# Two loads on SyncE's queue change places: half of the first pair's gate logits and the whole of the second pair's

## The chip, the cores and the metric

The kernel runs on one core of a Trainium2 chip. The metric is the device time of one execution in microseconds (us), the median of several executions. The profile is one further execution, taken by the hardware profiler.

## The reference

The program computes a gated linear recurrence over 768 time steps for 4 batches of 8 heads with 48 channels each, and behind it an MLP mixer over tokens and channels with 384 columns. Cut to what matters:

```
f = 1.0 / (1.0 + np.exp(-f_logit))                    # (4, 8, 768, 48)
for t in range(S):
    state = f[:, :, t, :, None] * state + np.einsum('bhd,bhe->bhde', k[:, :, t], v[:, :, t])
    y[:, :, t] = np.einsum('bhd,bhde->bhe', q[:, :, t], state)
x = y.transpose(0, 2, 1, 3).reshape(B, S, H * D)      # (4, 768, 384)
h = np.maximum(x.transpose(0, 2, 1) @ w_tok1, 0.0) @ w_tok2
u = x + h.transpose(0, 2, 1)
out = u + np.maximum(u @ w_ch1, 0.0) @ w_ch2
```

All inputs and the output are float32.

## The kernel before

**Tiling.** A batch of 768 steps is cut into six chunks of 128 steps, and the chunks are taken in three pairs, P = 0, 1, 2. In a pair, partition q of a tile holds the two neighbouring steps 2q and 2q+1, so a load of one pair brings runs of 96 elements. For each pair the kernel takes the gate logits f to the logarithm of the gate, `log(1 + exp(-f))`, on ScalarE; for the first two pairs of batch 0 this is one activation with the softplus table (line 454, in place in `f_sb`), for all later pairs an Exp and a Ln (lines 457 and 459). VectorE adds the two steps of each partition (`two`, line 448). TensorE sums over the steps with a triangular matrix (`sums`, line 479), and, for batch 0, takes the totals of the two chunks (`totals`, line 486). VectorE takes `first` from the sums (line 499), ScalarE makes the factors `GG` by Exp (lines 502 and 519), and VectorE multiplies q and k by them (`qk`, line 448 too, since it is a line of a helper). Then TensorE turns q and k (line 546), makes state contributions (`parts`, line 599), scores (line 581) and outputs (lines 657 and 665). The mixer follows: token layers (lines 709 and 725) and channel layers (lines 784 and 803), which are most of TensorE's work.

**Loads of batch 0.** Five loads come through the queues of SyncE (SP) and ScalarE (ACT) or GpSimd (POOL) at the start:

- the logits of pair 0 in two halves of four heads: `load_half(0, SP)` (192 KB in the profile's KB, line 348, SyncE's queue) and `load_half(1, ACT)` (the same line, ScalarE's queue). Both write the first pair's part of the tile `f_sb`; the first softplus needs both;
- the logits of pair 1, `load("f", 0, 1, SP)` (384 KB, line 357, SyncE's queue). The second softplus needs it;
- the logits of pair 2, `load("f", 0, 2, SP)` (384 KB, line 357, SyncE's queue), which is held back by a memset on POOL (`mark`, line 342);
- q, k and v of the three pairs, then the weights, all issued by POOL (lines 357, 418, 364), with a conversion to bf16.

Below, f1 is the load of pair 1's logits, half 0 and half 1 are the two halves of pair 0's, and f2 is the load of pair 2's.

**Order.** Every step of the program is an `Op` in a list. `ORDER`, written out by hand, is the order in which a planner (`Plan.best`) goes over them; each entry is four times an Op's number plus the choice of its engine. Op 2 is half 0 (entry 8), Op 3 is half 1 (entry 12) and Op 5 is f1 (entry 20). On one engine the steps are issued in the order of `ORDER`. The planner gives each Op a time on a clock of its own, from constants in the code; a load through SyncE's queue or a half through ScalarE's counts as landed a fixed time behind its issue:

```
HELD = (3850, 4300, 7100)                             # halves of pair 0, pair 1, pair 2
...
if e == PE and free[PE] < until and t - free[PE] > 270:
    n = int(t / 410) if not free[PE] else int((t - free[PE] - 50) / 215)
```

The times of this clock, in ns, decide two things that are in the program itself: which of the eight PSUM banks a step takes (the one that has been free longest by that clock), and, by the lines above, how many filler matmuls (`idle(n)`, line 852) TensorE is given ahead of a step that the planner sees waiting. The first such group stands ahead of the first pair's `sums`. In `idle(n)`, every four units are one float32 matmul of 512 columns, which the profile shows as two instructions, and each unit left over is one bf16 matmul of 512 columns.

In the kernel before, the first group is 14 units: three float32 matmuls (six instructions) and two bf16 ones.

Of the kernel before, what the change touches and what calls it, by code (L numbers as in the profile page):

```python
# [20 lines left out]
TURNED = 2  # L21
NQ = 2
ORDER = (
# [862 lines left out]
```

## Time and profile before

| | |
|---|---|
| time, median of 3 runs | 167.19 us (167.08 to 167.43) |
| time of the profiled execution | 167.07 us |
| its span, first to last instruction | 165.4 us |
| outside its span | 1.67 us |
| TensorE busy | 159.7 us (97% of the span) |
| VectorE busy | 128.5 us (78%) |
| ScalarE busy | 106.7 us (65%) |
| GpSimd busy | 61.7 us (37%) |
| granted TensorE clock | 1.00 |

In the lines of the profile PE is TensorE, PEld its weight loads, DVE VectorE, ACT ScalarE, POOL GpSimd, SP SyncE; a name with q behind it is that engine's queue of issues and waits. L454 is line 454 of the kernel. A line of the timeline has the start in us from the span's start, the duration of the group in us, engine, line, operation, what it writes and reads, the count, and in brackets the idle time just before and what ended it. Instructions that overlap in a pipeline are merged in such a group; a window that starts inside the group shows the later ones by themselves.

### The profile page before, as it was taken

How to read it: one execution, taken by the hardware profiler on the slowest of the kernel's cores; microseconds unless marked ns; L12 is line 12 of the kernel's file. 1: busy time of each engine (PE TensorE's matmuls, PEld its weight loads, DVE VectorE, ACT ScalarE, POOL GpSimd, SP SyncE). 2: the span in 40 equal slices, each digit the busy share in tenths (PEclk: the TensorE clock that was granted, in tenths of full speed). 3: DMA queues.
4: the chain of work that ended last, by engine and by line, in shares of the span. 5: the costliest groups of instructions: out<-in, count | busy, mean ns of one | idle time of the engine just before them, and what ended most of it. 6: DMA issues, size and time to landing. Idle time of an engine off the chain costs nothing.

```text
span 165.4 us, 4992 instructions
## 1 busy us (share of the span) xinstructions
PE 159.7 (97%) x2053; PEld 101.8 (62%) x2053; DVE 128.5 (78%) x284; ACT 106.7 (65%) x231; POOL 61.7 (37%) x86
## 2 busy tenths in 40 slices
PE   7999998999999999999999999999999999999992
PEld 3276665566666776666566766665667656565661
DVE  6558997589999999998999999988599526704331
ACT  3599785797899999999949966384812511623300
POOL 7970799954778610003904515200322020000000
DMA  4999999999999999566999990991900030680406
GB/s 110 221 179 171 200 212 240 176 209 225 220 226 222 225 244 142 96 87 127 141 214 121 144 125 0 108 213 49 222 6 4 0 65 10 182 319 20 175 32 206
DMA packets 68183, 24.34 MB, mean 147 GB/s; under 512 B 60896, under 2 KB 67296, under 8 KB 68160
## 3 DMA queue, kind: packets, MB, share of 16 engines
q0 software_dynamic: 41856, 13.77, 68.9%
q1 hardware_dynamic: 25776, 10.06, 29.1%
q8 instruction: 16, 0.26, 0.6%
q10 hardware_dynamic: 528, 0.20, 0.4%
q14 instruction: 7, 0.06, 0.1%
HBM read 25.17 MB, written 4.72 MB: 181 GB/s over the span
## 4 chain that ended last, share of the span: by engine, by line
PE 84%; DVE 3%; ACT 2%; issue 1%; DVEq 0%
PE ps L803 29%; PE ps L784 28%; PE ps L709 5%; PE ps L725 4%; PE ps L665 4%; PE ps L581 3%; PE ps L657 3%; PE ps L546 2%; PE ps L599 2%; PE ps L852 1%; PE ps L766 1%; PE ps L481 1%; PE ps L482 1%; DVE AmT L624 1%; DVE qk L448 1%
## 5 line engine op out<-in xcount | busy, mean ns | idle before, releaser
L803 PE MATMUL ps<-w_ch,zT 128*128 128x384 bf16 (+2 forms) x300 | 53.9, 320 | 0.0
L784 PE MATMUL ps<-uT,w_ch 128*128 128x384 bf16 x288 | 51.6, 326 | 0.0
L784 PEld LDWEIGHTS <-w_ch 128*128 128x128 bf16 x288 | 27.8, 98 | 17.6
L803 PEld LDWEIGHTS <-zT 128*128 128x128 bf16 x300 | 28.0, 98 | 17.1
L443 ACT ACTIVATE zT<-ps 128x384 bf16<-128x384 f32 x57 | 25.1, 493 | 16.3 <-PE ps L784 16.1
L624 DVE TENSOR_TENSOR AmT<-ps,mask 128x512 bf16<-128x512 f32 x44 | 28.6, 683 | 1.5 <-PE ps L581 1.2
L445 DVE TENSOR_SCALAR zT<-ps 128x384 bf16<-128x384 f32 x39 | 20.6, 551 | 10.0 <-PE ps L784 9.3
L814 DVE TENSOR_TENSOR x_nat<-x_nat,ps 128x384 f32<-128x384 f32 (+2 forms) x25 | 13.1, 532 | 10.5 <-PE ps L803 10.5
L438 POOL CAST state_bd<-state 48x192 bf16<-48x192 f32 x15 | 5.7, 377 | 28.8 <-DVE state L641 26.1
L502 ACT ACTIVATE GG<-ps 128x384 bf16<-128x384 f32 x24 | 11.0, 485 | 3.6 <-DVE first L499 2.9
L448 DVE TENSOR_TENSOR qk<-qk_sb,GG 128x768 bf16<-128x768 bf16 x24 | 12.8, 560 | 0.0
L357 POOL DMA_DIRECT2D v_sb<-in_v_dram x12 | 10.7, 894 | 5.3 <-DMA w_ch<-in_moe_w_ch_dram 3.4
L852 PE MATMUL ps<-steady 128*128 128x512 f32 (+1 forms) x21 | 11.5, 669 | 1.2 <-DVE steady L372 1.0
L519 ACT ACTIVATE GG<-first 128x384 bf16<-128x384 f32 x24 | 11.7, 518 | 0.2
L434 ACT ACTIVATE x_bf<-ps 128x384 bf16<-128x384 f32 x15 | 6.9, 483 | 7.4 <-PE ps L657 7.1
L741 DVE TENSOR_TENSOR x_nat<-x_nat,ps 128x384 f32<-128x384 f32 x21 | 10.6, 548 | 1.4 <-PE ps L725 1.2
L357 POOL DMA_DIRECT2D qk_sb<-in_k_dram x12 | 10.9, 904 | 1.7 <-POOLq L870 0.8
L434 ACT ACTIVATE u_bf<-x_nat 128x384 bf16<-128x384 f32 x12 | 5.8, 518 | 8.6 <-DVE x_nat L741 8.6
L357 POOL DMA_DIRECT2D qk_sb<-in_q_dram x12 | 10.8, 898 | 0.5 <-DMA qk_sb<-in_q_dram 0.3
L438 POOL COPY qT<-qJ 128x1024 bf16<-128x1024 bf16 x3 | 3.4, 1146 | 18.6 <-ACT zT L443 18.6
L709 PE MATMUL ps<-x_bf,w_tok 128*128 128x384 bf16 x48 | 10.3, 327 | 0.0
L434 ACT ACTIVATE x_nat<-ps 128x384 f32<-128x384 f32 x20 | 9.3, 491 | 0.1
(87 smaller groups left out, 230.8 us busy)
## 6 DMA issues: line engine op xcount, KB each, us to landing
out_dram<-x_nat SPq DMA_DIRECT2D x23, 192.0 KB, 2.2
f_sb<-in_f_logit_dram POOLq DMA_DIRECT2D x9, 384.0 KB, 8.8
qk_sb<-in_k_dram POOLq DMA_DIRECT2D x12, 192.0 KB, 8.6
qk_sb<-in_q_dram POOLq DMA_DIRECT2D x12, 192.0 KB, 8.7
v_sb<-in_v_dram POOLq DMA_DIRECT2D x12, 192.0 KB, 8.9
w_ch<-in_moe_w_ch_dram POOLq DMA_DIRECT2D x2, 576.0 KB, 9.1
w_ch<-in_moe_w_ch_dram POOLq DMA_DIRECT2D x1, 1152.0 KB, 10.3
f_sb<-in_f_logit_dram SPq DMA_DIRECT2D x2, 384.0 KB, 5.8
```

Source lines behind the costliest of these rows:

```text
L357: lambda eng=eng, into=held(dst[i], P), of=runs(src, b, P): eng.dma_start(out=into, in_=of),
L434: nc.scalar.activation(out_, in_, AF.Copy, bias=0.0, scale=1.0)
L443: nc.scalar.activation(out_, in_, AF.Relu, bias=0.0, scale=1.0)
L445: nc.vector.tensor_scalar(out_, in_, 0.0, None, ALU.max)
L448: (nc.vector if op.engine == DVE else nc.gpsimd).tensor_tensor(out_, a, b_, what)
L519: add(ACT, r, lambda n=n: nc.scalar.activation(GG[i][:, 0, n], first[i], AF.Exp, bias=0.0, scale=2.0 * n - 1.0), need=[("first", i)] + ([" ...
L624: add(DVE, r, lambda into=into, made=made, m4=m4: nc.vector.tensor_tensor(into, made(), m4, ALU.mult), need=masks, make=[("AmT", i, js, pa ...
L709: add(PE, rank("tok1", rt), lambda rt=rt, kt=kt, pm=pm: nc.tensor.matmul(banks[pm.at][:, 0:DM], lhsT=w_tok1[:, kt, rt * 128:(rt + 1) * 128 ...
L784: nc.tensor.matmul(banks[pm.at][:, 0:384], lhsT=w[:, kt, c0:c0 + 128], rhs=uT[:, th, :, kt, :], start=(kt == 0), stop=(kt == 2))
L803: nc.tensor.matmul(banks[pm.at][:, 0:n1 - n0], lhsT=zT[:, kt, tt * 128:(tt + 1) * 128], rhs=w_ch2[:, kt, n0:n1], start=(kt == 0), stop=(kt ...
L814: add(DVE, rank("ch2", tt), lambda un=un, pm=pm, n=n1 - n0: nc.vector.tensor_tensor(un, un, banks[pm.at][:, 0:n], ALU.add), make=[("x_nat" ...
L852: nc.tensor.matmul(banks[NBANK - 1], lhsT=one.broadcast_to((128, 128)), rhs=one.broadcast_to((128, 512)), start=True, stop=True)
```

## The change

Entries 20 (f1) and 8 (half 0) of `ORDER` change places. SyncE's queue is then given half 0 first and f1 behind it. No other entry moves, and no load changes its size, its tile or its queue.

```
 ORDER = (
-    0, 4, 12, 16, 24, 28, 32, 20, 8, 188, 192, 196, 36, 40, 44, 76, 68, 48, 52, 60, 208, 356, 212, 220, 64, 224,
+    0, 4, 12, 16, 24, 28, 32, 8, 20, 188, 192, 196, 36, 40, 44, 76, 68, 48, 52, 60, 208, 356, 212, 220, 64, 224,
```

Since the planner goes over `ORDER`, its clock is worked out anew with the two loads in their new places.

## The prediction

> **What bounds the kernel now.** I read the table of busy time by stretch first, to see where a start that comes earlier could still be lost (columns: stretch, its length, busy us and instructions of PE, PEld, DVE, ACT, POOL, the granted clock, the DMA share, GB/s).
>
> ```profile
> 0.00:8.00 8.00, 6.98 (x10) 2.45 (x10) 4.96 (x27) 3.48 (x4) 6.81 (x14) 1.00 1.05 165
> 34.00:160.00 126.00, 126.00 (x1596) 80.59 (x1594) 102.25 (x212) 82.79 (x184) 35.32 (x51) 1.00 0.89 134
> ```
>
> From 34 to 160 us TensorE has no idle time: 126 us of 126. There the end is set by TensorE's work and by when that work begins, so whatever moves the state of the program at 34 us moves the end by as much. The question is what sets the time before 34.
>
> The timeline of the first 11 us answers it, engine by engine. First the three issues and ScalarE, with the time from issue to landing of the three loads from the DMA view (the second of its rows is half 0; the third, from a window that ends ahead of the other issues, is f1).
>
> ```profile
> 0.81 0.48 ACTq L348 DMA_DIRECT2D f_sb<-in_f_logit_dram  x1
> 0.81 0.47 SPq L357 DMA_DIRECT2D f_sb<-in_f_logit_dram  x1
> 1.34 0.60 SPq L348 DMA_DIRECT2D f_sb<-in_f_logit_dram  x1
> 5.79 1.58 ACT L454 ACTIVATE f_sb<-f_sb 128x768 f32<-128x768 f32 x2 [3.19 <-DMA f_sb<-in_f_logit_dram]
> 6.54 0.83 ACT L454 ACTIVATE f_sb<-f_sb 128x768 f32<-128x768 f32 x1
> 7.38 1.28 ACT L841 ACT_TABLE_LOAD   x1
> 8.82 0.49 ACT L502 ACTIVATE GG<-ps 128x384 bf16<-128x384 f32 x1 [0.15 <-DVE first L499]
> 9.20 0.93 ACT L519 ACTIVATE GG<-first 128x384 bf16<-128x384 f32 x2
> ```
> ```profile
> f_sb<-in_f_logit_dram ACTq DMA_DIRECT2D x1, 192.0 KB, 4.2
> f_sb<-in_f_logit_dram SPq DMA_DIRECT2D x1, 192.0 KB, 4.4
> f_sb<-in_f_logit_dram SPq DMA_DIRECT2D x1, 384.0 KB, 4.4
> ```
>
> Half 1 lands at 0.81 + 4.2 = 5.0, f1 at 0.81 + 4.4 = 5.2, half 0 at 1.34 + 4.4 = 5.74. The first softplus needs both halves and starts at 5.79, right behind half 0. The load that is needed first lands last, while f1, needed second, waits 0.54 us in the tile. ScalarE's 3.19 us of idle time end on that load.
>
> Then VectorE and TensorE behind it (the rows of TensorE are from windows that begin inside its groups, so that each start can be read).
>
> ```profile
> 6.66 0.56 DVE L448 TENSOR_TENSOR two<-f_sb 128x384 f32<-128x384 f32 x1 [1.22 <-ACT f_sb L454]
> 7.39 0.56 DVE L448 TENSOR_TENSOR two<-f_sb 128x384 f32<-128x384 f32 x1 [0.18 <-ACT f_sb L454]
> 8.22 0.56 DVE L499 TENSOR_TENSOR first<-ps,f_sb 128x384 f32<-128x384 f32 x1 [0.27 <-PE ps L479]
> 9.80 0.56 DVE L499 TENSOR_TENSOR first<-ps,f_sb 128x384 f32<-128x384 f32 x1 [0.91 <-PE ps L486]
> 10.27 1.02 DVE L448 TENSOR_TENSOR qk<-qk_sb,GG 128x768 bf16<-128x768 bf16 x2
> ```
> ```profile
> 0.99 6.26 PE L852 MATMUL ps<-steady 128*128 128x512 f32 x8 [0.99 <-DVE steady L372]
> 6.28 0.98 PE L852 MATMUL ps<-steady 128*128 128x512 bf16 x2
> 6.70 0.55 PE L852 MATMUL ps<-steady 128*128 128x512 bf16 x1
> 7.28 1.65 PE L479 MATMUL ps<-two,tri 128*128 128x384 f32 x4
> 7.70 1.22 PE L479 MATMUL ps<-two,tri 128*128 128x384 f32 x3
> 8.03 0.90 PE L479 MATMUL ps<-two,tri 128*128 128x384 f32 x2
> 8.44 0.49 PE L479 MATMUL ps<-two,tri 128*128 128x384 f32 x1
> 8.76 1.89 PE L486 MATMUL ps<-ones,two 128*128 128x64 f32 x16
> ```
>
> Two legs run to the first `qk` at 10.27. One: second softplus 6.54, `two` 7.39, sums of the second pair 8.03, its totals 8.76, its `first` 9.80, and `qk` 0.47 us behind it in VectorE's order. The other: table load to 8.66, GG at 8.82 behind the first pair's `first` (8.22), and the two Exps that end at 9.20 + 0.93 = 10.13. They meet within 0.14 us, so both must come earlier. From `qk` on the chain of waits runs through VectorE and ScalarE to TensorE's channel layers with no load named as a releaser.
>
> **The change part by part.** *The loads.* No byte and no issue is added; SyncE issues the same two loads, the second 0.5 to 0.6 us behind the first as now, and f2 behind them waits for POOL's memset either way. What moves is the order in which SyncE's queue (q1) is drained; ScalarE's is q10, POOL's q0. The DMA view for windows from 0 to 3.25, 4.5 and 5.25 gives packets so far:
>
> ```profile
> q1 hardware_dynamic: 419, 0.16, 26.5%
> q10 hardware_dynamic: 12, 0.00, 0.5%
> ...
> q1 hardware_dynamic: 993, 0.38, 36.6%
> q10 hardware_dynamic: 505, 0.19, 15.3%
> ...
> q1 hardware_dynamic: 1554, 0.59, 45.7%
> q10 hardware_dynamic: 528, 0.20, 13.6%
> q0 software_dynamic: 82, 0.02, 3.5%
> ```
>
> q10's 528 packets are all of half 1, so a half is 528 and f1 about twice that. In q1 the first 528 packets, now half 0's, are through between 3.25 and 4.5 (at an even pace 3.25 + 1.25 x 109 / 574 = 3.49); before, half 0 was the last third, through at about 5.3, and landed 0.45 us later. So half 0 will land at 3.9 to 4.2, ahead of half 1, whose queue I leave as it is: 5.0. The first softplus then starts at 5.0 + 0.05 = 5.05 in place of 5.79, a gain of 0.74. f1 becomes the last third: its last packets go at 5.3, and with a tail between 0.45 (half 0's) and 0.65 (f1's now: its packet 1040 at about 4.55, landing 5.2) it lands at 5.75 to 5.95. The second softplus can follow the first after the pitch 6.54 - 5.79 = 0.75, at 5.80; so it starts at 5.80 to 6.00 in place of 6.54. The gain there is 0.54 to 0.74 and cannot be more, since one softplus must still follow the last landing where two did.
>
> *The filler matmuls.* The wording hides a second edit. The planner's clock puts half 0 at 3850 in place of 4280, so its first softplus moves from 4318 to 3888, `two` from 5196 to 4766, and the first `sums` from 5801 to 5371; int(5371 / 410) = 13 where it was 14. This is a count written into the program, no time of the chip. Thirteen units are three float32 and one bf16 matmul: one bf16 filler less. It matters: with 14, TensorE would be in fillers until about 6.70 + 0.42 = 7.12 and the sums, at 7.28 now, would gain 0.16 at most. With 13 they can start at 6.70. On paper the clock's lead of 430 is 195 at the second pair's sums, 10 at the first `parts` (values taken as landed at 10350) and 74 behind; the next two filler counts stay at 4 (4.50 before rounding in both) and 8 (8.87 and 8.56), and the bank picks that I followed, to 17 us of that clock, stay. Later picks may differ: bounded by one eviction more or less in a row of two, 0.5 us to either side (the 0.49 of the GG row), taken as 0 because a pick by longest-free seldom binds.
>
> *The sums.* The first pair's `two` would start at 5.05 + (6.66 - 5.79) = 5.92 and end at 6.48, so the sums would start when the fillers are done, 6.70, a gain of 0.58. Two bounds for the rest. The granted clock reads 1.00 in the first 8 us, but the fillers' pace does not bear it out: the bf16 filler at 6.28 took 0.42 to the next. The four float32 pieces of the sums take 0.42, 0.33, 0.41, 0.32: the first piece of each pair is the long one, whichever pair it is, so by 7.28 the array was at its full pace already, and up to 6.70 it ran at about half pace (a float32 filler piece took about 0.88, six of them from 0.99 to 6.28; the two at 10.49, quoted next, took 1.08 together). The switch lay between 6.70 and 7.28. At 6.70: the pieces start at 6.70 and 7.12 and the second pair's at 7.45. At 7.28: the first piece does 0.58 / 0.84 of its work by 7.28 and ends at 7.41, the second at 7.74. The second pair's sums, at 8.03 now, so start at 7.45 to 7.74, a gain of 0.29 to 0.58 (`two` is there by 7.45). Half-way, with the switch at 6.99: the first piece does 0.29 / 0.84 = 0.35 of its work by then, ends at 6.99 + 0.65 x 0.42 = 7.26, the second at 7.59, a gain of 0.44. I take 0.44, since no row divides the interval.
>
> ```profile
> 10.49 1.08 PE L852 MATMUL ps<-steady 128*128 128x512 f32 x2
> ```
>
> *The two legs.* Totals, `first` and `qk` follow the second pair's sums in fixed steps: 0.44. On the other leg the first pair's `first` gains 0.44 as well (7.59 against 8.03 at the end of its sums), and the table load ends 0.54 to 0.74 earlier, which hides under it. So `qk` starts at 9.83.
>
> *What could be late next.* Of the loads behind it, the first pair's v has the tightest use, the first `parts`.
>
> ```profile
> 3.57 0.91 POOL L357 DMA_DIRECT2D v_sb<-in_v_dram  x1
> 11.95 0.43 PE L599 MATMUL ps<-v_sb,qk 64*64 64x48 bf16 x16
> ```
> ```profile
> v_sb<-in_v_dram POOLq DMA_DIRECT2D x1, 192.0 KB, 7.5
> ```
>
> It lands at 3.57 + 7.5 = 11.07 and is used at 11.95, a cover of 0.88, which outlasts even 0.74; past 0.88 it would eat the rest. So 0.44 goes through to 34 us and to the end. The profiled execution's 167.07 becomes 166.63; the median of the runs lies 0.12 above that execution, 167.19, and becomes 166.75. Rounded between them: **166.7**.
>
> **The rivals.** *The array is at full pace already.* Were the switch to come before 6.5, the fillers would end sooner, the first sums would follow `two` at 6.54, and only f1 would bound: gain 0.54 to 0.74, say 0.65, 166.5 against the median. For it: nothing ties the switch to the program in this one trace. Against: here it fell after 6.70, on this program's start. The Trainium skill, "TensorE: Matmul & The Clock Gate", section on the HAM clock gate, says that the window of about 3.4 us in which activity is judged runs free of the kernel's start, and that the transition varies with where the first matmul falls in it; the half-pace fillers here agree, while a single trace cannot show that it varies. Chance 0.25.
>
> *No change to be seen.* Half 1 may land later than 5.0, since both halves are now moved first and side by side; if it came at 5.5, the first softplus would start at 5.55, the second at 6.30, and the gain would be 0.24; with the switch at 7.28 and any slip beside it the 0.29 falls under the bound as well. 166.9 to 167.2. For it: q10 had its first packets only at 3.25, behind q1. Against: q10 went from 12 to 505 packets while q1 was busy throughout. A measurement of this kernel can tell about 0.2%, 0.33 us, from no change. Chance 0.18.
>
> *Slower: f1 now ends in POOL's traffic.* q0 starts at about 5.1 (82 packets by 5.25, in the rows above). A load of the same size that ran beside it is f2.
>
> ```profile
> f_sb<-in_f_logit_dram SPq DMA_DIRECT2D x1, 384.0 KB, 7.1
> ```
>
> If f1 took 7.1 from its issue at 1.41, it would land at 8.5, the second softplus start at 8.55 in place of 6.54, and with it the table load that every Exp waits for: +2.0, 169.2. The point from which it decides is a landing later than 6.5; half-way between 5.85 and 8.5, 7.2, it costs 0.7, 167.9. Against it: all of q1 was through at 5.3 when f1 went first, and the bytes are the same. Chance 0.08; with the later bank picks going the wrong way, 0.14 for slower in all.
>
> **How the numbers follow.** The forecast has 0.43, the fast array 0.25, no change 0.18, slower 0.14. The forecast's own range, gain 0.29 to 0.58, lies between 166.6 and 166.9 against the median, its lower end just under the bound, so I count 0.39 of it as faster and the rest as same: faster 0.64, same 0.22, slower 0.14. The range goes from the fast array on the profiled execution's time, 167.07 - 0.74 = 166.33, less a tenth for the spread of the runs, to 167.4, the slowest run shown, which leaves out the dear end of f1's delay: 166.2 to 167.4.
>
> **What would show it.** Right: one filler instruction less in the first group (seven); the first softplus at 5.0 or a little before, the second at 5.8 to 6.0; the landing of half 0 before half 1 and of f1 at 5.75 to 5.95; the first sums at 6.70; `qk` at about 9.8; TensorE's stretch without idle time beginning, and the span ending, about 0.44 earlier. Wrong: eight fillers; a second softplus behind 6.5; a first `qk` that is early and an end where it was all the same, which would mean a wait between them that this trace does not name; or idle time on TensorE after 34.

## Result and the profile after

The changed kernel takes 165.98 us in the median of 20 runs (165.81 to 169.14), the kernel before 167.28 us beside it (20 runs, 166.74 to 170.87). The ratio is 0.9946, with a 95% interval from 0.9926 to 0.9967: faster by 0.5%. The ratio agrees with that of the means, 166.27 and 167.17, from which three executions over 1.5% above the fastest of their kernel are left out (169.14, and 170.86 and 170.87 before); the medians lie 0.8% apart, since the changed kernel's few long executions weigh on its mean and not on its median. The forecast, 166.7 with a range from 166.2 to 167.4, said faster and was too small: it gave 0.44 us where the means differ by 0.90 and the medians by 1.30. The median lies 0.22 below the range. The ratio, taken on the 167.19 from which the forecast started, gives 166.29, just inside it, and that is partly luck: what holds it there are those long executions, which the forecast did not have.

The profiled execution of the changed kernel took 167.62 us and is one of its slowest, so its rows show which steps moved, but its end is no measure of the gain. A copy of the changed kernel was therefore profiled too (166.35 us; below "the copy").

The instructions differ from those of before as said: SyncE's two loads have changed places and TensorE has one bf16 filler, a weight load and a matmul, less. The issue order of ScalarE, VectorE and GpSimd is the same.

The timeline of the profiled execution of the changed kernel, its first 12 us:

```profile
0.81 0.48 ACTq L348 DMA_DIRECT2D f_sb<-in_f_logit_dram  x1
0.81 0.46 SPq L348 DMA_DIRECT2D f_sb<-in_f_logit_dram  x1
1.34 2.68 SPq L357 DMA_DIRECT2D f_sb<-in_f_logit_dram  x2
1.00 4.75 PE L852 MATMUL ps<-steady 128*128 128x512 f32 x7 [1.00 <-DVE steady L372]
4.51 0.84 ACT L454 ACTIVATE f_sb<-f_sb 128x768 f32<-128x768 f32 x1 [1.91 <-DMA f_sb<-in_f_logit_dram]
5.38 0.56 DVE L448 TENSOR_TENSOR two<-f_sb 128x384 f32<-128x384 f32 x1
5.70 0.84 ACT L454 ACTIVATE f_sb<-f_sb 128x768 f32<-128x768 f32 x1 [0.35 <-DMA f_sb<-in_f_logit_dram]
6.00 0.91 PE L479 MATMUL ps<-two,tri 128*128 128x384 f32 x2 [0.25 <-DVE two L448]
6.56 1.28 ACT L841 ACT_TABLE_LOAD   x1
6.57 0.56 DVE L448 TENSOR_TENSOR two<-f_sb 128x384 f32<-128x384 f32 x1 [0.63 <-ACT f_sb L454]
7.93 1.90 PE L486 MATMUL ps<-ones,two 128*128 128x64 f32 x16
10.85 1.03 DVE L448 TENSOR_TENSOR qk<-qk_sb,GG 128x768 bf16<-128x768 bf16 x2 [1.32 <-DMA qk_sb<-in_q_dram]
12.26 0.43 PE L599 MATMUL ps<-v_sb,qk 64*64 64x48 bf16 x16
```

The two softplus are now apart, each with a wait for a load in brackets: the first starts at 4.51 in place of 5.79, the second at 5.70 in place of 6.54. Seven filler instructions stand where eight did. Every step up to the totals is early, the first `two` by 1.28 and the totals (7.93 in place of 8.76) by 0.83. Then comes what spoilt this execution: `qk` waits 1.32 us for q and starts at 10.85, later than the 10.27 of before.

The DMA view of the same execution, from issue to landing (first half 1, half 0 and f1, then the first q):

```profile
f_sb<-in_f_logit_dram ACTq DMA_DIRECT2D x1, 192.0 KB, 3.7
f_sb<-in_f_logit_dram SPq DMA_DIRECT2D x1, 192.0 KB, 3.4
f_sb<-in_f_logit_dram SPq DMA_DIRECT2D x1, 384.0 KB, 4.3
qk_sb<-in_q_dram POOLq DMA_DIRECT2D x1, 192.0 KB, 8.4
```

Half 0 lands at 4.2, half 1 at 4.5, f1 at 1.34 + 4.3 = 5.64. The q issued at 2.34 lands at 2.34 + 8.4 = 10.74; before it took 6.4 and landed at 8.7. In the other executions of the changed start that were profiled it took 5.4 to 6.3.

The copy's timeline, ScalarE, VectorE and TensorE:

```profile
1.00 5.79 PE L852 MATMUL ps<-steady 128*128 128x512 f32 x7 [1.00 <-DVE steady L372]
4.29 0.84 ACT L454 ACTIVATE f_sb<-f_sb 128x768 f32<-128x768 f32 x1 [1.69 <-DMA f_sb<-in_f_logit_dram]
5.36 0.54 DVE L448 TENSOR_TENSOR two<-f_sb 128x384 f32<-128x384 f32 x1
5.48 0.84 ACT L454 ACTIVATE f_sb<-f_sb 128x768 f32<-128x768 f32 x1 [0.35 <-DMA f_sb<-in_f_logit_dram]
6.36 0.56 DVE L448 TENSOR_TENSOR two<-f_sb 128x384 f32<-128x384 f32 x1 [0.45 <-ACT f_sb L454]
6.63 1.46 PE L479 MATMUL ps<-two,tri 128*128 128x384 f32 x4
7.47 0.56 DVE L499 TENSOR_TENSOR first<-ps,f_sb 128x384 f32<-128x384 f32 x1 [0.56 <-PE ps L479]
7.92 1.89 PE L486 MATMUL ps<-ones,two 128*128 128x64 f32 x16
9.43 1.01 DVE L448 TENSOR_TENSOR qk<-qk_sb,GG 128x768 bf16<-128x768 bf16 x2
```

Here q is in time and the first `qk` starts at 9.43, 0.84 earlier than before. The sums stand right behind the fillers, with no wait named, though the first `two` was done at 5.90. So in this execution the fillers held the first sums, as the forecast said. In the execution above, the same seven fillers were through at 5.75 and the sums followed `two`.

The tables of busy time by stretch (columns as in the prediction), the changed kernel and then the copy:

```profile
34.00:160.00 126.00, 126.00 (x1597) 80.61 (x1594) 102.30 (x213) 83.32 (x185) 35.59 (x52) 1.00 0.88 135
```
```profile
34.00:160.00 126.00, 126.00 (x1595) 80.66 (x1594) 101.73 (x210) 82.09 (x183) 34.42 (x50) 1.00 0.87 133
```

TensorE is without idle time from 34 to 160 us in both, as before. From the first matmul of line 784 to the start of the last two additions of line 814 there are 128.31 to 128.38 us in all 14 profiled executions. What reaches the channel layers early is early at the end, whole.

### The profile page after: what moved, and what is told of

Same layout as the page of the kernel before. It is cut to its first block, busy times and chain, and to the rows that moved or that the text cites. A ratio compares the mean times of both kernels' runs of the same rounds, so it can differ in the third digit from the quotient of the medians.

```text
span 165.9 us, 4990 instructions
## 1 busy us (share of the span) xinstructions
PE 158.6 (96%) x2052; PEld 101.4 (61%) x2052; DVE 128.8 (78%) x284; ACT 106.9 (64%) x231; POOL 61.7 (37%) x86
## 4 chain that ended last, share of the span: by engine, by line
PE 82%; DMA 5%; ACT 4%; DVE 4%; issue 1%; POOL 1%; DVEq 0%; ACTq 0%; POOLq 0%
PE ps L803 28%; PE ps L784 28%; DMA qk_sb<-in_q_dram 5%; PE ps L709 5%; PE ps L725 4%; PE ps L665 3%; PE ps L581 3%; PE ps L657 2%; PE ps L546 2%; PE ps L599 2%; PE ps L766 1%; PE ps L481 1%; ACT state_bd L434 1%; ACT x_nat L434 1%; DVE qk L448 1%
## 5 line engine op out<-in xcount | busy, mean ns | idle before, releaser
L357 POOL DMA_DIRECT2D v_sb<-in_v_dram x12 | 10.7, 894 | 6.3 <-DMA w_ch<-in_moe_w_ch_dram 3.7
L852 PE MATMUL ps<-steady 128*128 128x512 f32 (+1 forms) x20 | 9.8, 610 | 1.0 <-DVE steady L372 1.0
```

What stands on the lines that cost most here:

```text
L357: lambda eng=eng, into=held(dst[i], P), of=runs(src, b, P): eng.dma_start(out=into, in_=of),
```

## The experiments

All use the median of several runs beside runs of the kernel before on the same chip. Theory A in the expectations is that of the prediction: the last landing of the logits, with one softplus behind it, and the fillers' count where they hold the sums.

**The copy.** No edit; a second profile.

> The changed kernel once more, for a second profile of it. Theory A (one softplus in place of two behind the last landing): the second softplus starts at 5.6 to 5.8 as in the first profile, 0.8 ahead of the kernel before; if the first pair's q lands before 9.4, the first qk starts at 9.4 to 9.5 and the span is about 164.2 (time 165.85); if q lands later, qk waits for it and the time is longer by as much (the first profile: 1.32 of wait, 167.62). Theory B (the spread of the runs comes from the time at which the array reaches full pace, not from q): a slower run would show late sums and no wait for q.

Measured: 165.85 us (165.6 to 166.38, 6 runs), ratio 0.9919 [0.9905, 0.9933]. The late q of the first profile is no part of the change. Two executions of one program differ in how long the fillers take (to 5.75 and to 6.79), and in when q lands (10.7 and 7.8).

**The loads alone: fourteen fillers kept.**

```
 (changed kernel)
-n = int(t / 410) if not free[PE] else int((t - free[PE] - 50) / 215)
+n = 14 if not free[PE] else int((t - free[PE] - 50) / 215)
```

> The changed order of loads, but with 14 units in the first group of fillers as before. Theory A: the order of the loads carries the gain; where the array is at full pace from about 4.5, the fillers end by 6.0 and the 14th costs 0 to 0.2, so the time is within 0.2 of the changed kernel; where the array stays slow to 6.7 or later, the sums start at 7.1 and the time is about 0.3 to 0.4 longer. Theory C (the shorter fillers carry the gain): the time goes back to that of the kernel before.

Measured: 166.56 us (166.02 to 166.87, 6 runs), ratio 0.9956 [0.9944, 0.9968]. So the order of the loads alone gives 0.44% (0.32 to 0.56), and theory C, by which the time would go back to that of before, fails. It is more than half of what the copy gains on the same chip, and those two intervals do not overlap; but the 20 runs of the changed kernel (0.9926 to 0.9967) overlap with this one, so what the fourteenth unit costs is not settled. The profile of this kernel shows a first `qk` at 9.28, earlier than the copy's, because its array ran fast sooner. It is the fastest of its six runs. What it lost again stands in its timeline, at the weight load of the first `parts`:

```profile
5.53 0.84 ACT L454 ACTIVATE f_sb<-f_sb 128x768 f32<-128x768 f32 x1 [0.39 <-DMA f_sb<-in_f_logit_dram]
9.28 1.02 DVE L448 TENSOR_TENSOR qk<-qk_sb,GG 128x768 bf16<-128x768 bf16 x2
11.17 0.33 PEld L599 LDWEIGHTS <-qk 64*64 64x64 bf16 x16 [0.32 <-DMA v_sb<-in_v_dram]
```

The first v lands at 11.17, and `parts` wait 0.32 us for it. The prediction gave v a cover of 0.88 and said that a gain past that would be eaten: the gain here is 0.99, and the second `qk`, 13.58, has only 0.75 of it. In the copy, v landed 0.6 earlier and nothing waited.

**Thirteen and twelve fillers without the new order; the count alone; a copy of before.** Four kernels ask whether the filler matters by itself. The third cuts one bf16 filler into two matmuls of 256 columns, so that columns fall to thirteen units while the count of instructions stays.

```
 (kernel before)
+n = 13 if not free[PE] ...        # first kernel
+n = 12 if not free[PE] ...        # second
+n = 13, its one bf16 filler as 2 x 256 columns   # third
```

> The kernel before with 13 units in the first group of fillers, its loads in the old order. Theory A: no difference (ratio 0.999 to 1.001), since the first sums wait for the first pair's two, which ends at 7.2, and not for the fillers. Theory C: the full gain, a ratio of 0.994 to 0.996.

> The kernel before with twelve filler units in place of fourteen. Its sums wait for the tile two (7.32 us in the profile with thirteen units), not for the filler. Theory A, data bound: no reason for any gain, and an earlier end of the filler may even cost by a later switch to full pace; ratio 0.999 to 1.003. Theory G, instruction count: the gap moves by one matmul more and out of the third pair's outputs, and the gain of 0.2 per cent stands or grows, ratio 0.995 to 0.998. Theory S, spread alone: 0.998 to 1.000 with no order between twelve, thirteen and fourteen.

> The kernel before, with the filler's columns cut to thirteen units but its matmul count kept as with fourteen (one bf16 filler is cut into two matmuls of 256 columns). Theory F, the filler's time: the block on TensorE ends earlier by one unit, so the time is that of the kernel before with thirteen units, ratio 0.997 to 0.999, about 166.95. Theory G, the instruction count: what thirteen units gained came from two instructions fewer ahead of the gap in the third pair's outputs (0.61 us before, no reason shown), so this kernel is as the kernel before, ratio 1.000 within 0.001, and its gap stands after the 30th matmul of that line.

> A copy of the kernel before: its profile is a second execution of the same program. If the switch of TensorE to full pace is set by the program, the sums' four 384-column matmuls run as in the first profile; if it differs between executions, as it did between two executions of the changed kernel, the first qk moves by up to 0.6 us around 10.27. Ratio 1.000 within 0.002; the gap in the third pair's outputs stands after the 30th matmul again, its length between 0.3 and 0.7 us.

Measured: thirteen, 166.93 us (166.62 to 167.46, 11 runs), 0.998 [0.997, 0.9991]; twelve, 166.91 us (166.78 to 168.57, 12 runs), 0.9998 [0.9978, 1.0018]; split, 167.41 us (166.78 to 168.42, 12 runs), 1.002 [0.9998, 1.0041]; the copy of before, 167.38 us (167.06 to 167.6, 12 runs), 1.0011 [0.9999, 1.0023]. There is no order in these. Against theory F, the kernel with thirteen units' columns has no gain; against G's size, twelve is not faster than thirteen. The 0.2% of the first stays without a cause: twelve, which should have more of it, has none, and a bare copy reads 0.1% off to the other side. So in the kernel before the filler count does nothing that could be shown, as theory A has it. The timeline of the copy of before shows why:

```profile
1.00 4.78 PE L852 MATMUL ps<-steady 128*128 128x512 f32 x8 [1.00 <-DVE steady L372]
7.21 1.65 PE L479 MATMUL ps<-two,tri 128*128 128x384 f32 x4 [1.43 <-DVE two L448]
10.20 1.02 DVE L448 TENSOR_TENSOR qk<-qk_sb,GG 128x768 bf16<-128x768 bf16 x2
```

The fillers were done at 5.78 here and at 7.25 in the first profile of the same program, and `qk` moved by 0.07, as much as the softplus did (5.72 for 5.79). The sums wait 1.43 us for `two`. My expectation of up to 0.6 us from the array's pace was wrong for this kernel: the pace does differ, but nothing hangs on it.

**Twelve fillers, and the split filler, with the new order.** The same edits in the changed kernel.

> The changed kernel with 12 units in the first group, no bf16 filler at all. Theory F: where the array is slow to 6.7 or later the sums start at 6.3 in place of 6.7, so the time falls by another 0.2 to 0.4 in most runs: a ratio of 0.989 to 0.992; where it is fast from 4.5 to 5, nothing changes. If the gap left between the fillers and the sums (two ends at 5.9 to 6.0) kept the array slow for longer, the sums' pieces would take 0.8 each and the time would rise by 0.3 or more. The gap in line 665 falls behind the 32nd matmul or at the next group's first by theory G.

> The changed kernel with 13 units of filler, the last bf16 filler cut into two matmuls of 256 columns: the columns of 13 units, but as many TensorE instructions as with 14. Theory F (fillers cost their time: the first sums wait for them): as the changed kernel, a ratio of 0.991 to 0.995. Theory G (the number of TensorE instructions counts, since it shifts the place in the program at which TensorE stands 0.3 to 1.1 us without a shown reason inside the third pair's outputs, line 665): as with 14 units, 0.995 to 0.997, and the gap falls between the 30th and the 31st of these matmuls in place of the 31st and 32nd.

Measured: twelve, 165.95 us (165.72 to 166.13, 6 runs), 0.9925 [0.9909, 0.9941]; split, 166.0 us (165.68 to 167.34, 12 runs), 0.9939 [0.9918, 0.996]. Both lie with the copy; a thirteenth unit no longer costs anything that shows. The split filler has the count of fourteen units and, by its median, the time of thirteen, which would put the price of fourteen on the fillers' time and not on their count; but its interval overlaps that of fourteen, and this is not settled.

**The first pair's softplus second, in the kernel before.** ScalarE takes the second pair's logits first, which lie waiting, so that one softplus follows the last landing there too.

```
 (kernel before; 47, 48: the two softplus)
-return sorted(done, key=lambda op: op.start)
+return sorted(done, key=... 47 and 48 exchanged ...)
```

> The kernel before, loads in the old order and 14 units of filler, but ScalarE takes the second pair's softplus first (f1 lands at 5.2) and the first pair's behind it. The last landing, half 0 at 5.74, then has one softplus behind it, as in the changed kernel, and the table load ends 0.5 earlier; but the sums keep their order, first pair first, and its two now ends at 7.4 to 7.5 in place of 7.2. Theory A in the form of the prediction (the leg by way of the sums binds): slower by 0.1 to 0.3, a ratio of 1.000 to 1.002. Theory T (the leg by way of the table load alone binds): faster by 0.4 to 0.5, 0.997.

Measured: 167.41 us (166.75 to 168.26, 12 runs), 1.0022 [1.0004, 1.0039]. No gain. Its timeline:

```profile
5.15 1.58 ACT L454 ACTIVATE f_sb<-f_sb 128x768 f32<-128x768 f32 x2 [2.55 <-DMA f_sb<-in_f_logit_dram]
6.75 1.28 ACT L841 ACT_TABLE_LOAD   x1
7.38 1.56 PE L479 MATMUL ps<-two,tri 128*128 128x384 f32 x4 [1.48 <-DVE two L448]
8.92 0.49 ACT L502 ACTIVATE GG<-ps 128x384 bf16<-128x384 f32 x1 [0.89 <-DVE first L499]
```

The table load is 0.63 earlier than before, but the sums come 0.10 later, since the first pair's `two` now stands behind both softplus, and GG waits 0.89 us for the first pair's `first`. The first `qk` is at 10.29. An early table load alone brings nothing: the first pair has to be early as well, which the order of loads gives.

**GpSimd's loads for the first pair ahead of f2.** In the changed kernel, the memset that holds back f2 is issued behind the first v, so that q, k and v meet less traffic; with thirteen and with twelve fillers.

```
 (changed kernel; 20, 21: mark and f2, 22: the first v)
-return sorted(done, key=lambda op: op.start)
+return sorted(done, key=lambda op: self.ops[22].start + 1.0 if op in (self.ops[20], self.ops[21]) else op.start)
```

> The changed kernel with the memset that holds f2 back put behind the issue of the first pair's v on POOL, so that f2 is issued at about 4.5 in place of 3.6. Theory D (f2's packets on SyncE's queue delay the last packets of q on POOL's queue, and that makes the spread): q lands at 8.9 or earlier, qk at 9.4 to 9.5 without a wait, the time 165.8 to 165.9 in nearly all runs, median 0 to 0.2 below the changed kernel; f2 lands at 11.0 to 11.8, ahead of its Exp. Theory E (q's late landing has nothing to do with f2): q lands anywhere between 8.7 and 10.8 and the runs spread from 165.8 to 167.8 as those of the changed kernel do.

> The changed kernel with f2's memset put behind the issue of the first pair's v, and 12 units of filler: the two edits together. Theory D and F: no run waits for q, and the sums follow two at 6.0 to 6.3: 165.3 to 165.9, a ratio of 0.988 to 0.992, and the runs within 0.5 of each other but for the gap in line 665.

Measured: 165.9 us (165.77 to 166.12, 4 runs), 0.9916 [0.9903, 0.9928]; with twelve fillers 165.62 us (165.35 to 165.97, 6 runs), 0.991 [0.9892, 0.9928]. With f2 late, v landed 6.3 and 5.9 us after its issue, in place of 7.0 to 8.2 in the five profiled executions with the new order and f2 early, and nothing waited for it. The first q took 5.6 and 5.5, much as in the copy (5.5). Whether f2 had to do with the late q of the first profile (theories D and E) is not settled: the copy and the twelve fillers, with f2 early, had no run above 166.4 us among six each either. The second kernel is the fastest version by its median, though its interval and the copy's overlap.

**f1 over two queues.** The kernel with twelve fillers and the late f2, with f1 asked for as two halves. The edit is for f1 alone, and f1 is issued behind half 1 on ScalarE's queue.

```
 (f1 only)
-eng.dma_start(out=into, in_=of)
+nc.sync.dma_start(out=into[:, 0:HP], in_=of[:, 0:HP])
+nc.scalar.dma_start(out=into[:, HP:H], in_=of[:, HP:H])
```

> The changed kernel with the second pair's mark and third logits' load issued behind the first v, twelve filler units, and the second pair's logits asked for as two halves, on SyncE's and ScalarE's queues behind the first pair's halves. Theory A, the last landing of the logits binds the second softplus (ScalarE waits 0.35 us for it in the changed kernel): with half of it behind each queue it lands up to 0.35 us earlier, the second softplus starts at 5.05 to 5.3, and the time is 165.3 to 165.6. Rival B, the bytes are the same and both queues share the engines: the landing stays at 5.4 to 5.65 and the time is that without the split, 165.6, ratio 0.989 to 0.993.

Measured: 165.68 us (165.46 to 165.97, 6 runs), 0.9918 [0.9901, 0.9934]. The second softplus:

```profile
5.47 0.84 ACT L454 ACTIVATE f_sb<-f_sb 128x768 f32<-128x768 f32 x1 [0.36 <-DMA f_sb<-in_f_logit_dram]
```

It waits as long as in the copy and starts at 5.47, against 5.40 without the split. That is as rival B has it: in these two executions a second queue for the same bytes did not bring the last landing of the logits forward.

**The runs added up.** One thing besides the start moves the time from one execution to the next. In all 14 profiled executions TensorE pauses once in the third pair's outputs, for 0.24 to 1.07 us, with no releaser shown. The rows of four of them (before, the copy, fourteen fillers, twelve fillers, all but the first with the new order):

```profile
26.84 0.20 PE L665 MATMUL ps<-v_sb,AmT 64*128 64x48 bf16 x2 [0.61 <-issue]
```
```profile
26.26 0.18 PE L665 MATMUL ps<-v_sb,AmT 64*128 64x48 bf16 x1 [0.89 <-issue]
```
```profile
25.72 0.20 PE L665 MATMUL ps<-v_sb,AmT 64*128 64x48 bf16 x2 [0.31 <-issue]
```
```profile
26.00 0.50 PE L657 MATMUL ps<-state_bd,qT 128*128 128x96 bf16 x8 [0.72 <-issue]
```

From the first `qk`, this pause and the profiled execution's own time:

| kernel | second softplus | first `qk` | pause | time | time - `qk` - pause |
|---|---|---|---|---|---|
| before | 6.54 | 10.27 | 0.61 | 167.07 | 156.19 |
| before, its copy | - | 10.20 | 0.64 | 167.09 | 156.25 |
| before, softplus exchanged | - | 10.29 | 0.32 | 166.75 | 156.14 |
| before, 13 fillers | - | 10.32 | 1.07 | 167.46 | 156.07 |
| before, 13 split | - | 10.30 | 0.55 | 166.99 | 156.14 |
| before, 12 fillers | - | 10.22 | 0.61 | 166.78 | 155.95 |
| changed | 5.70 | 10.85 | 0.99 | 167.62 | 155.78 |
| changed, its copy | 5.48 | 9.43 | 0.89 | 166.35 | 156.03 |
| changed, 14 fillers | 5.53 | 9.28 | 0.31 | 166.02 | 156.43 |
| changed, 13 split | 5.48 | 9.23 | 0.64 | 165.99 | 156.12 |
| changed, f2 late | 5.53 | 9.28 | 0.43 | 165.77 | 156.06 |
| changed, 12 fillers | 5.58 | 9.33 | 0.72 | 166.00 | 155.95 |
| 12 fillers, f2 late | 5.40 | 9.15 | 0.24 | 165.35 | 155.96 |
| the same, f1 split | 5.47 | 9.22 | 0.34 | 165.46 | 155.90 |

The last column lies between 155.90 and 156.25 but for two executions: fourteen fillers, which waited 0.32 us for v, and the first profile of the changed kernel, where the delay by q is made up in part (the second `qk`, at 14.64, follows the first after 3.79, in the copy after 4.05). So the first `qk`, the pause and the landings of q and v account for the differences of the profiled times to within about 0.2 us to either side. What is left goes with the number of TensorE's instructions, in the old order and in the new: 156.12 to 156.25 with fourteen units and with the split filler, which has their count, 156.03 to 156.07 with thirteen, 155.90 to 155.96 with twelve. Why is not shown. Where the second softplus is read, the first `qk` follows it after 3.73 before and 3.75 in the changed kernels but for the copy (3.95), whose sums were held by fillers, and the execution that waited for q.

## Why the prediction was right, and where its size was not

**The bound.** Right. The end follows the start of the channel layers, and that follows the first `qk` and the pause: 128.31 to 128.38 us from line 784 to the last additions of line 814, whatever the kernel.

**The landings.** Half 0 was forecast at 3.9 to 4.2 and came at 4.2 in the first profile and 4.0 in the copy. Half 1 was to stay at 5.0 and came at 4.5 and 4.3; I had left ScalarE's queue as it was. Packets so far, up to 3.25 us, in the profiled execution of the changed kernel:

```profile
q1 hardware_dynamic: 418, 0.16, 21.6%
q10 hardware_dynamic: 157, 0.06, 7.4%
```

SyncE's queue had come as far as before (419), while ScalarE's had moved 157 packets in place of 12. Over all profiles it is 12 to 33 in the six with the old order and 157 to 280 in the eight with the new: here the half on ScalarE's queue starts earlier when the load asked for beside it is a half and not f1. By 5.0 us the same counts read 1506 in q1 for 1407 before. So f1, forecast at 5.75 to 5.95, landed at 5.64 and in the copy at 5.44. The first softplus came at 4.51 and 4.29 for 5.05, and `two` at 5.38 and 5.36 for the 5.92 forecast: in the first profile it follows the softplus after 0.87, as before, while in the copy VectorE was busy with constants until 5.36, and part of the lead was lost.

**The second softplus: the term that was mis-sized.** I wrote that the gain there is 0.54 to 0.74 and cannot be more, since one softplus must still follow the last landing. The reason holds: the pitch of one softplus is 0.75. But it took the last landing as fixed, and the last landing moved forward too, from 5.74 to 5.64 and 5.44. The gain was 0.84 in the first profile and 1.06 in the copy.

**The fillers.** Seven instructions, as forecast. That the count matters only with the new order is borne out: in the kernel before twelve, thirteen and fourteen cannot be told apart, with the new order fourteen is slower than the copy's thirteen by 0.37% of the time before, with intervals that do not overlap, though the interval of the changed kernel's own 20 runs overlaps with that of fourteen. That the time goes into holding the sums is shown for an execution like the copy's (thirteen); the profiled execution with fourteen ran fast early and lost its share to v. The other thing that the planner's clock could have moved, the PSUM banks, did not move: worked through, the planner gives every step the same bank in both kernels.

**The sums.** I took the switch of the array to full pace as half-way between 6.70 and 7.28, which gave 0.44, the smallest term, and let it set the sum. In the copy the fillers run nearly as late as in that picture, and the sums start at 6.63 (forecast 6.70), but all four then run at 0.32 to 0.33 apart, 6.63, 6.95 and the last at 7.60. So full pace was there by 6.63, and the 0.42 of each pair's first piece, which I had read as its own length, was 0.33 in a row without a wait. The term comes out as 0.58 for a switch at the sums' start, 0.07 for the earlier start and twice 0.09 for the pieces: 0.83, against 0.84 measured at the totals and at `qk`. In the first profile and in the kernels with twelve fillers the sums were not held by fillers at all. That is the rival "the array is at full pace already", to which I gave 0.25 and 166.5 us, and it is the commoner case in the changed executions that were profiled: all but the copy have `qk` 3.75 behind the second softplus or, in the first profile, totals 2.23 behind it as before (8.76 - 6.54 = 2.22).

The Trainium skill, "TensorE: Matmul & The Clock Gate", section on the HAM clock gate, calls the window free-running and the number of slow matmuls variable from run to run. These traces agree: the eight fillers of one program ended at 7.25 in one execution and at 5.78 in another, the seven of the changed one at 5.75 and 6.79, while the granted clock in the rows of these stretches reads 1.00 throughout.

**What could be late next.** Right, and it decides more than I gave it. With a gain of 0.84 to 1.12 at the first `qk` the cover of 0.88 for v is about used up: 0.32 us of waiting with fourteen fillers, none in the copy. I did not list q, which landed at 8.7 before, used at 10.27; in the first profile it came at 10.74 and cost the whole gain and more (first `qk` 10.85). That fits the changed kernel's runs, ten of which lie between 165.81 and 165.87 while four lie above 167; that those four are late loads too is argued, since only one of them was profiled.

**From 0.84 to 1.30.** The copy's profiled execution is 0.72 faster than the first profile of before: 0.84 at `qk`, 0.28 back in a longer pause (0.89 for 0.61), and 0.16 by the last column of the table, which is lower for fewer filler instructions (156.14 to 156.25 with fourteen units on the old order, 155.95 with twelve). The medians differ by more, 1.30. A changed execution with `qk` at 9.28, as two other kernels show (three more lie between 9.22 and 9.33), and the pause of before, would come to 156.03 + 9.28 + 0.61 = 165.92, near the median of 165.98. That most runs of the changed kernel look like this is an estimate from these rows; no run of that cluster was profiled.

**The rivals that fell.** The half did not land late, so "no change" had no ground; f1 was nearly through when GpSimd's traffic began (by 5.0 us SyncE's queue had moved 1506 packets and GpSimd's 58), so "slower" had none either. A slow single execution came by a load that I had not named.

## What to carry to other kernels

When two loads exchange places in a queue, work out both landings anew, and also those of the queue beside it: here a smaller load in front let the neighbour start earlier, and the last landing itself moved. A filler or any step that is hidden under a wait shows no price; it may have one when the wait is gone, so try it again after the change, in both kernels. Before reading one profiled execution as the kernel, profile a copy: here two executions of one program differed by 1.27 us, as much as the change was worth.

## What was not expected of the hardware

A pause of 0.24 to 1.07 us stands on TensorE in the third pair's outputs in all 14 executions. Its place moves with the count of TensorE's instructions: behind the 30th matmul of line 665 with the count of fourteen filler units (the split filler too), behind the 31st with thirteen, and one further on, behind the 32nd and ahead of line 657, with twelve, whatever the loads do. Where the first `qk` is the same (10.27 to 10.32), 0.32, 0.61 and 1.07 of pause go with 166.75, 167.07 and 167.46 us, so its length reaches the end whole. Runs of the kernel before gather near 166.76, 167.08 and 167.42 us, with some between.

The DMA records of the same traces offer a cause. Beside the queues of the loads the page lists one of the kind "instruction":

```profile
q8 instruction: 16, 0.26, 0.6%
```

Its 16 packets are of 16 KB each. In the three executions just named TensorE reaches the pause at nearly the same time, 26.2 to 26.3. A packet of q8 ends ahead of it at 25.26, 25.52 and 25.94, and the pause ends at 26.52, 26.84 and 27.33: the later the packet, the longer the pause. In all 14 executions the pause ends 1.21 to 1.51 us behind the end of that packet, while it begins anywhere from 0.31 to 1.13 behind it. So the pause looks like a wait for the next block of TensorE's instructions, which also fits a place that goes by their count. That q8 feeds TensorE is read from this fit alone; why the packet comes when it does, and why TensorE goes on only 1.2 us or more behind it, no run shows.

The first q took 8.4 us from issue to landing in one execution and 5.4 to 6.7 in the others, with the same loads in the same order or nearly so; the profile shows the wait and not its cause.
